# Moving two weight transfers of a kernel's opening from SyncE's queue to ScalarE's

## The chip, the cores and the metric

The kernel runs on one core of a Trainium2 chip. The metric is the device time of one execution in microseconds. Two scales appear: the timed value (343.01 us for the profiled run of the kernel before) and the span of the trace, from its first to its last instruction (341.22 us for the same run). A transfer is *issued* by the sequencer of an engine and has *landed* with the last of the sixteen semaphore updates ("marks" below) that a trace records for it; what needs its data can start then. TensorE is PE, its weight loads PEld, ScalarE ACT, VectorE DVE, SyncE SP; "SPq" and "ACTq" are the sequencers that issue transfers.

## The reference

Two independent attention blocks, A and B, side by side. Each projects 512 tokens to 32 heads of 128, attends over cached keys and values (4 key heads, 8 query heads each), and projects back. bfloat16 throughout.

```python
q = (x @ wq).reshape(B, Sq, Hq, Dh).transpose(0, 2, 1, 3)   # x: 16 x 32 x 1024, wq: 1024 x 4096
scores = einsum("bhqd,bhkd->bhqk", q, repeat(k_cache)) * Dh ** -0.5
o = einsum("bhqk,bhkd->bhqd", softmax(scores), repeat(v_cache))
out = o.transpose(0, 2, 1, 3).reshape(B, Sq, Hq * Dh) @ wo
# the outputs of A and B are concatenated
```

## The kernel before

Only the opening matters: the query projection of A's first eight heads. x has eight chunks of 128 columns; chunks 0 to 3 are loaded plainly and transposed on TensorE, chunks 4 to 7 are transposed by DMA. "Row r" below means rows r*128 to r*128+127 of wq, six heads wide (128 partitions x 768 elements, 192 KB). `NF` is 6, `HC` 4, `TT` 4, `DC` 8.

```python
def load_x(d0, t0, t1, eng=nc.sync):
    eng.dma_start(out=x_sb[:, t0:t1, d0 * P:(d0 + 2) * P],
                  in_=x_v[:, t0:t1, d0 * P:(d0 + 2) * P])

def load_w0(d0, d1, h0, h1):
    nc.sync.dma_start(out=w0[d0 // HC][:, d0 % HC:(d1 - 1) % HC + 1, h0 * DH:h1 * DH],
                      in_=wq_v[:, d0:d1, h0 * DH:h1 * DH])

load_x(0, TT // 2, TT, nc.scalar)          # x chunks 0, 1: second half of the tokens
nc.scalar.preload_act_table_set("natural_log_exp_and_others")
load_x(0, 0, TT // 2)                      # x chunks 0, 1: first half
load_w0(0, 1, 0, NF // 2)                  # first row, first half
load_w0(0, 1, NF // 2, NF)                 # first row, second half
load_w0(1, 2, 0, NF)                       # second row
load_x(2, 0, TT)                           # x chunks 2, 3
load_w0(2, 3, 0, NF)                       # third row
load_w0(3, 4, 0, NF)                       # fourth row
load_w0(0, HC, NF, REP)                    # heads 6, 7 of the first four rows
# ... the rest of the weights, x's chunks 4 to 7, keys and values, all on nc.sync
# ...
warm_up(22)
for k, ts in enumerate(((0, TT // 2), (TT // 2, TT))):
    transpose_x(0, *ts, nc.vector.tensor_copy)
    transpose_x(1, *ts, nc.scalar.copy, spare[k])
for ts in ((0, TT // 2), (TT // 2, TT)):
    first_heads(range(0, NF // 2), (0,), *ts)      # first row, first half
first_heads(range(NF // 2, NF), (0,))              # first row, second half
first_heads(range(0, NF - 2), (1,))                # second row, four heads
transpose_x(2, 0, TT, nc.vector.tensor_copy)       # x chunk 2
transpose_x(3, 0, TT, nc.scalar.copy)              # x chunk 3
first_heads(range(NF - 2, NF), (1,))               # second row, two heads
first_heads(range(NF), (2, 3))                     # third and fourth row
# ...
```

TensorE runs these in this order, so each transfer has a moment by which it must have landed.

Of the kernel before, what the change touches and what calls it, by code (L numbers as in the profile page):

```python
# [181 lines left out]
def kernel(  # L182
# [14 lines left out]
    nc = tc.nc  # L197
# [20 lines left out]
    def fast_path(ok_i):  # L218
        with ExitStack() as fctx:
# [235 lines left out]
            NF = REP - 2  # L455
# [8 lines left out]
            def load_x(d0, t0, t1, eng=nc.sync):  # L464
                eng.dma_start(
                    out=x_sb[:, t0:t1, d0 * P:(d0 + 2) * P],
                    in_=x_v[:, t0:t1, d0 * P:(d0 + 2) * P],
                )
# [4 lines left out]
                    in_=A_x.flatten_outer_dims()[:, d0 * P:(d0 + 2) * P],  # L473
                )

            def load_w0(d0, d1, h0, h1):
                nc.sync.dma_start(
                    out=w0[d0 // HC][:, d0 % HC:(d1 - 1) % HC + 1, h0 * DH:h1 * DH],
                    in_=wq_v[:, d0:d1, h0 * DH:h1 * DH],
                )  # L480

            load_x(0, TT // 2, TT, nc.scalar)
            nc.scalar.preload_act_table_set("natural_log_exp_and_others")
            load_x(0, 0, TT // 2)
            load_w0(0, 1, 0, NF // 2)
            load_w0(0, 1, NF // 2, NF)
            load_w0(1, 2, 0, NF)
            load_x(2, 0, TT)
            load_w0(2, 3, 0, NF)
            load_w0(3, 4, 0, NF)  # L490
            load_w0(0, HC, NF, REP)
            load_w0(HC, HC + 1, 0, REP)
# [182 lines left out]
    ok_i = flag.tile([1, 1], I32, name="ok_i")  # L675
    total = 2 * 2 * NG * QW
    ok = fast_path(ok_i)
    with tc.If(ok < total, preferred_fallthrough_block=True, label="general"):
        general_path(tc, problems, out_flat)
# [30 lines left out]
```

## Time and profile before

| | before |
|---|---|
| timed, median of 3 before the prediction | 343.63 us (343.56 to 343.73) |
| span of the profiled run | 341.22 us |
| TensorE busy | 335.2 us, 98% |
| first matmul of the main stream (line 301) | 18.91 us |

The lines that carry this are in the prediction below. A row of the timeline merges like instructions; its busy time hides gaps shorter than the modelled length of a matmul, so distances between starts are quoted from single records.

### The profile page before, as it was taken

How to read it: one execution, taken by the hardware profiler on the slowest of the kernel's cores; microseconds unless marked ns; L12 is line 12 of the kernel's file. 1: busy time of each engine (PE TensorE's matmuls, PEld its weight loads, DVE VectorE, ACT ScalarE, POOL GpSimd, SP SyncE). 2: the span in 40 equal slices, each digit the busy share in tenths (PEclk: the TensorE clock that was granted, in tenths of full speed). 3: DMA queues.
4: the chain of work that ended last, by engine and by line, in shares of the span. 5: the costliest groups of instructions: out<-in, count | busy, mean ns of one | idle time of the engine just before them, and what ended most of it. 6: DMA issues, size and time to landing. Idle time of an engine off the chain costs nothing.

```text
span 341.2 us, 5454 instructions
## 1 busy us (share of the span) xinstructions
PE 335.2 (98%) x2082; PEld 213.6 (63%) x2121; DVE 265.5 (78%) x336; ACT 185.9 (54%) x209; POOL 46.7 (14%) x206
## 2 busy tenths in 40 slices
PE   8999999999999999999999999999999999999996
PEld 6455666666666666666666666666666666666555
DVE  1046988888988898888888988879888888889540
ACT  3058666666667667666645545555555555555110
POOL 0001110011111111110012221222122101111100
PEclk9999999999999999999999999999999999999999
DMA  7999999999996987899999955998449997430001
GB/s 211 287 190 273 285 249 202 233 242 268 291 248 154 232 242 219 210 314 299 308 306 258 250 125 144 334 268 242 118 103 296 356 187 176 104 97 16 18 18 33
DMA packets 128094, 71.70 MB, mean 210 GB/s; under 512 B 75840, under 2 KB 127296, under 8 KB 128064
## 3 DMA queue, kind: packets, MB, share of 16 engines
q1 hardware_dynamic: 127264, 70.07, 84.1%
q0 software_dynamic: 384, 1.05, 0.9%
q8 instruction: 17, 0.28, 0.3%
q10 hardware_dynamic: 416, 0.20, 0.2%
q14 instruction: 13, 0.11, 0.1%
HBM read 50.86 MB, written 2.10 MB: 155 GB/s over the span
## 4 chain that ended last, share of the span: by engine, by line
PE 98%; issue 1%; ACT 0%; ACTq 0%
PE f_ps L320 32%; PE q_ps L301 28%; PE ob L425 17%; PE s_ps L357 16%; PE q_ps L534 4%; PE q_ps L516 1%; PE xT_ps L524 0%; ACT o_sb L329 0%; ACTq L329 0%
## 5 line engine op out<-in xcount | busy, mean ns | idle before, releaser
L365 ACT ACTIVATE p_sb<-s_ps,shift 128x1024 bf16<-128x1024 f32 x128 | 142.7, 1115 | 97.5 <-PE s_ps L357 88.1
L376 DVE TRANSPOSE_TENSOR_REDUCE parts<-p_sb 128x32 f32<-128x1024 bf16 x128 | 158.7, 1240 | 21.0 <-ACT p_sb L365 19.3
L320 PE MATMUL f_ps<-wo_sb,oT 128*128 128x512 bf16 (+1 forms) x525 | 128.2, 366 | 0.6
L301 PE MATMUL q_ps<-xT,wq_sb 128*128 128x512 bf16 x430 | 113.2, 379 | 0.5
L425 PE MATMUL ob<-p_sb,v_sb 128*128 128x256 bf16 x512 | 76.8, 273 | 0.8
L357 PE MATMUL s_ps<-qT,kT 128*128 128x256 bf16 x512 | 76.8, 273 | 0.0
L320 PEld LDWEIGHTS <-oT 128*128 128x128 bf16 x544 | 53.2, 98 | 35.3
L357 PEld LDWEIGHTS <-kT 128*128 128x128 bf16 x512 | 56.9, 113 | 28.3
L301 PEld LDWEIGHTS <-wq_sb 128*128 128x128 bf16 x448 | 43.8, 98 | 32.2
L425 PEld LDWEIGHTS <-v_sb 128*128 128x128 bf16 x512 | 50.1, 98 | 20.0
L447 DVE TENSOR_TENSOR oT<-r,ob 128x512 bf16<-128x512 f32 x64 | 43.9, 686 | 19.9 <-PE ob L425 19.4
L411 DVE STREAM_TRANSPOSE r<-rall 128x512 f32<-128x512 f32 x64 | 44.2, 691 | 1.1
L309 ACT CAST qT<-q_ps 128x512 bf16<-128x512 f32 x56 | 32.7, 583 | 16.5 <-PE q_ps L301 16.5
L394 POOL COPY half<-cs 64x32 f32<-64x32 f32 x32 | 6.5, 204 | 231.8 <-DVE cs L384 231.8
L329 ACT CAST o_sb<-f_ps 128x512 bf16<-128x512 f32 (+1 forms) x17 | 9.5, 559 | 23.6 <-PE f_ps L320 23.6
L534 PE MATMUL q_ps<-xT,w_sb 128*128 128x512 bf16 (+1 forms) x65 | 14.4, 379 | 0.1
L384 DVE TENSOR_REDUCE cs<-parts 128x32 f32<-128x128 f32 x32 | 12.1, 377 | 1.1
L406 DVE RECIPROCAL rall<-sums 128x32 f32<-128x32 f32 x32 | 10.2, 319 | 3.3 <-POOL sums L403 3.3
L534 PEld LDWEIGHTS <-w_sb 128*128 128x128 bf16 x67 | 6.8, 102 | 7.0 <-DMA w_sb<-in_A_wq_dram 0.2
L560 DVE CAST qT<-q_ps 128x512 bf16<-128x512 f32 x4 | 2.5, 684 | 10.2 <-PE q_ps L534 10.2
L331 POOL DMA_DIRECT2D out_dram<-o_sb x8 | 4.6, 574 | 29.3 <-ACT o_sb L329 29.3
L395 POOL TENSOR_TENSOR half<-half,cs 64x32 f32<-64x32 f32 x32 | 7.8, 243 | 2.6
(25 smaller groups left out, 44.7 us busy)
## 6 DMA issues: line engine op xcount, KB each, us to landing
v_sb<-in_A_v_cache_dram SPq DMA_DIRECT2D x16, 512.0 KB, 5.7
wq_sb<-in_B_wq_dram SPq DMA_DIRECT2D x8, 1024.0 KB, 5.7
wo_sb<-in_A_wo_dram SPq DMA_DIRECT2D x8, 1024.0 KB, 7.4
v_sb<-in_B_v_cache_dram SPq DMA_DIRECT2D x16, 512.0 KB, 4.7
wo_sb<-in_B_wo_dram SPq DMA_DIRECT2D x8, 1024.0 KB, 8.1
wq_sb<-in_A_wq_dram SPq DMA_DIRECT2D x5, 1024.0 KB, 5.8
wq_sb<-in_A_wq_dram SPq DMA_DIRECT2D x2, 512.0 KB, 6.7
kT<-in_A_k_cache_dram SPq DMA_TRANSPOSE x64, 4.4
```

What stands on the lines that cost most here:

```text
L301: nc.tensor.matmul(ps[:], lhsT=w[:, dc, (h % 4) * DH:(h % 4 + 1) * DH], rhs=xT[pr][:, dc, :], start=(dc == 0), stop=(dc == DC - 1),)
L309: nc.scalar.copy(out=qT[pr, g][:, :, hl, :], in_=ps[:].rearrange("p (b s) -> p b s", s=SQ),)
L320: nc.tensor.matmul(ps[:, 0:width], lhsT=oT[pr, tt][:, h, :], rhs=wo_tiles[pr, nh, h // REP][:, h % REP, off:off + width], start=(h == 0), ...
L357: nc.tensor.matmul(s_ps[:, c, :], lhsT=kT[:, i % GRP, c, :], rhs=qT[pr, g][:, b, :, :].rearrange("p h s -> p (h s)"), start=True, stop=True,)
L365: nc.scalar.activation(out=p_sb[:], in_=s_ps[:], func=ACTF.Exp, bias=shift[:], scale=SCALE)
L376: nc.vector.tensor_reduce(out=parts[k][:, q, :, :].rearrange("p c h -> p (c h)"), in_=st[i]["p"][:].rearrange("p c (h s) -> p (c h) s", s=SQ),
L384: nc.vector.tensor_reduce(out=cs[:], in_=parts.pop(k)[:].rearrange("p q c h -> p q h c"), axis=AX.X, op=ALU.add,)
L406: nc.vector.reciprocal(out=rall[:, k, :], in_=quad.pop(k)[:])
L411: nc.vector.transpose(out=r[:].rearrange("p n s -> p (n s)"), in_=rall[:, k, o * 2 * REP:(o + 1) * 2 * REP] .unsqueeze(2).to_broadcast([P, ...
L425: nc.tensor.matmul(ob[j][:, q, :], lhsT=v_sb[:, i % GRP, c, :], rhs=st[i]["p"][:, c, :], start=(c == 0), stop=(c == KC - 1),)
L447: nc.vector.tensor_tensor(out=out, in0=rcp.pop(j)[:].rearrange("p (q h) s -> p q h s", h=REP), in1=ob.pop(j)[:].rearrange("p q (h s) -> p ...
L534: nc.tensor.matmul(first_q[h][:, ts], lhsT=w0[dc // HC][:, dc % HC, h * DH:(h + 1) * DH], rhs=xT[0][:, dc, ts], start=(dc == 0 and t0 == 0 ...
```

## The change

The intent: SyncE issues one transfer each 0.47 us or so, and the opening's transfers stand in its queue. ScalarE has only its part of x and a table load to do at first. Giving it the second and third rows should bring these sooner, and let SyncE get on about a microsecond earlier.

```diff
-            def load_w0(d0, d1, h0, h1):
-                nc.sync.dma_start(
+            def load_w0(d0, d1, h0, h1, eng=nc.sync):
+                eng.dma_start(
...
             load_w0(0, 1, NF // 2, NF)
-            load_w0(1, 2, 0, NF)
+            load_w0(1, 2, 0, NF, nc.scalar)
             load_x(2, 0, TT)
-            load_w0(2, 3, 0, NF)
+            load_w0(2, 3, 0, NF, nc.scalar)
             load_w0(3, 4, 0, NF)
```

## The prediction

> **What bounds the kernel now.** I read the head of the page first, then the chain of waits, then only the first ten microseconds, since every moved transfer belongs to the opening.
>
> From the page of the kernel before:
>
> ```profile
> span 341.2 us, 5454 instructions
> PE 335.2 (98%) x2082; PEld 213.6 (63%) x2121; DVE 265.5 (78%) x336; ACT 185.9 (54%) x209; POOL 46.7 (14%) x206
> ...
> PE 98%; issue 1%; ACT 0%; ACTq 0%
> ```
>
> The second line gives each engine's busy time, the third the chain of work that ended last. TensorE is busy 335.2 of 341.2 us and is 98% of that chain; no transfer appears in it. A transfer that lands earlier can pay only where TensorE waits for it. So I listed all waits of TensorE's weight loads over the whole span:
>
> ```profile
> PEld L516 <- issue: 0.9, 1, 0.9
> PEld L534 <- DMA w_sb<-in_A_wq_dram: 0.2, 1, 0.2
> ```
>
> Columns: who waited, for what, total us, times, longest. One weight load in the whole program waits for a weight transfer, 0.2 us. That is a row the change moves, so the hope behind the change has a target. The timeline shows whether those 0.2 us reach the matmuls (start, length, engine, line, out<-in, count, idle time before it):
>
> ```profile
> 0.93 2.52 PE L516 MATMUL q_ps<-const-bfloat16-1.0 128*128 128x128 bf16 x22 [0.93 <-PEq L694]
> ...
> 3.28 1.09 PE L524 MATMUL xT_ps<-ident,x_sb 128*128 128x128 bf16 x8
> ...
> 4.17 2.79 PE L534 MATMUL q_ps<-xT,w_sb 128*128 128x256 bf16 x13
> ...
> 5.79 0.67 PEld L534 LDWEIGHTS <-w_sb 128*128 128x128 bf16 x4 [0.20 <-DMA w_sb<-in_A_wq_dram]
> ...
> 6.79 0.61 PE L524 MATMUL xT_ps<-ident,x_sb 128*128 128x128 bf16 x8
> ...
> 7.45 11.62 PE L534 MATMUL q_ps<-xT,w_sb 128*128 128x512 bf16 x52
> ```
>
> None of these matmul rows has an idle time but the first. In the single records the distances between matmul starts tell more than the busy rows. Around the waiting load, matmuls start at 5.710, 5.925, 6.141, 6.357 us: each 0.215 us after the last, the undisturbed distance of a 512-column matmul in this trace. The load ran beside the previous matmul, so its 0.2 us cost nothing. Real losses before 8 us are three:
>
> - the first transpose of x at 3.276 instead of 3.241 (0.035 us; SyncE's half of x landed at 3.23),
> - the fifth at 3.763 instead of 3.678 (0.085 us; ScalarE's half landed at 3.72),
> - 0.024 us at 7.690, where the matmul waits for VectorE's copy of the third x chunk.
>
> The other gaps near 0.22 us later on are each one missing matmul record. So TensorE is paced by its own instructions from 4.165 us to the end.
>
> **How tight each row is.** From issue, landing and first weight load (single records and issues of the trace):
>
> - first row, first half (96 KB): issued 1.26, landed 3.92, loaded at 4.06: 0.14 us to spare
> - first row, second half (96 KB): 1.75, 5.03, 5.17: 0.14
> - second row (192 KB): 2.22, 5.75, 5.79: none for the load, which still kept pace
> - x chunks 2 and 3 (256 KB): 2.69, 6.55, 6.59: almost none
> - third row (192 KB): 3.17, 7.06, 7.45: 0.4
> - fourth row (192 KB): 3.71, 7.77, 8.77: 1.0
> - everything behind: 0.9 us or more (the next block landed 9.13, its matmuls start near 10.05).
>
> The order was already tuned to arrive just in time. The change touches the tight ones.
>
> **What the Trainium skill says.** "DMA: Bandwidth & Descriptors", section "Issuing engines are not separate DMA queues", says that DMAs started from several engines run on the same 16 engines and interleave, and that this saves only issue time. The trace agrees: the two x halves are issued side by side (0.74 and 0.82 us, 0.45 and 0.46 us long), but SyncE's packets start at 1.83 and ScalarE's only at 2.51 us, when SyncE's are nearly done. "Perfetto Trace Analysis", section "Sequencer Loop", says engine instructions are pushed into a queue while the sequencer goes on reading. The trace agrees for short waits: at 338.24 us ScalarE's sequencer finishes a semaphore wait inside its cast of 338.22 to 338.59. No record shows a DMA issued during a table load. "ScalarE: Activation LUTs", section "What ACT_TABLE_LOAD costs", gives about 1283 ns for the load, and this trace has 1.28 us, from 1.31 to 2.60; the drain that it adds is not visible here, since ScalarE's next instruction waits for TensorE. "TensorE: Matmul & The Clock Gate", Part 1, says matmuls run at half clock until about 4 us of activity; here 256-column starts lie 0.213 us apart until 5.02 us, and 512-column ones 0.215 us apart from about 5.3 us, so the full rate comes about 4.1 us after the first warm-up matmul at 0.93.
>
> **The change part by part.** TensorE, VectorE and GpSimd keep the same instructions in the same order. SyncE loses two issues; ScalarE gains two, behind its x half and the table load. In the listing of the changed program the transfers keep their places in the ring of eight completion semaphores, so the waits are the old ones.
>
> 1. SyncE saves 0.476 us before x chunks 2 and 3 (2.690 less 2.215) and 0.547 us more before the fourth row (the spacing 3.166 to 3.713): 1.02 us for all behind. All these were hidden: gain on the path 0.
>
> 2. The second and third rows' issue on ScalarE. If the sequencer passes the table load, they go at about 1.31 and 1.78 us instead of 2.22 and 3.17. Landings come 0.5 to 1 us sooner, and the 0.2 us wait of the load may vanish: gain 0, since the matmuls kept pace.
>
> 3. Contention for the first row. Its second half (issued 1.75) would now have the second row's 192 KB beside or ahead of it. DMA was not full there: 117 and 163 GB/s in 3.5 to 4.5 us, where 348 GB/s is reached in 5.0 to 5.5. Estimate from these: 96 + 96 + 192 KB from its first packet at 2.89 us at some 300 GB/s take 1.3 us, so all three end near 4.2; landings trail most of the packets by 0.6 to 0.8 us, giving 4.8 to 5.0. Serial handling as between the two x halves could add 0.65 us (192 KB at 300 GB/s) to the 5.03: at worst 5.6 against a need of 5.17. I take 5.2 to 5.4 as likely, a stall of 0 to 0.25 us. The first half, if pushed back 0.1 us, has 0.14 to spare.
>
> 4. x's own halves are issued before everything moved, so the two losses of 0.035 and 0.085 us remain. At most 0.024 us can come back at 7.690, and that needs an earlier copy, while its transposes keep their place: 0.
>
> Sum: 0 gained, about 0.1 us lost in the mean: 343.63 + 0.1 = 343.73, rounded up slightly for the second rival.
>
> **The rivals.**
>
> *A small gain.* The labelled 0.2 us wait could be taken at face value: 343.4. For it: it is the only transfer wait of TensorE's weight loads. Against it: the even 0.215 us distances across it, and the start still hangs on x.
>
> *ScalarE's sequencer waits out the table load.* Then the rows go at about 2.60 and 3.07 us. The second row is issued 0.38 us later than before and behind x chunks 2 and 3, now issued at 2.22. It would land 0.4 to 0.8 us later than 5.75, or 0.4 to 0.8 us of stall with nothing else to absorb it: 344.0 to 344.4. Separate queues would soften this. The copies of xT on ScalarE, first due at 3.92, would still be free of it: two issues of about 0.47 us end near 3.55. I give this 30%, because the trace has no DMA beside a table load.
>
> *Contention as in part 3 at its worst.* 0.45 us on the first row's second half: 344.1. For it: the serial packets of the two x halves. Against it: the DMA engines' share was only 0.53 at 3.5 to 4.0 us.
>
> *A reordering far downstream.* Buffers and waits are unchanged, TensorE never waits for data later, so no cost beyond the opening has anything to hang on.
>
> **Range and chances.** The three runs before differ by 0.17 us. All mechanisms lie between -0.15 us (all three start-up losses gone) and +0.8 us; 2% is 6.9 us, over eight times the largest of them. I predict 343.8 us, 343.3 to 344.4, and leave 1% for each side of the 2% band.
>
> **What would show each step.** Issue times of the second and third rows on ScalarE: near 1.3 and 1.8 us (part 2) or near 2.6 and 3.1 (rival). The first row's second half landing before 5.17 us means no stall; later shows part 3. A gap over 0.215 us between matmul starts from 5.1 to 6.6 us is the whole change in time. SyncE's fourth-row issue should come at about 2.69. The start of the first 512-column q_ps matmul of the main stream (18.9 us) should move by the same amount as the span. What would make me wrong: a change of span without such a gap in the opening, an earlier landing of x itself, or a full clock that comes at another time because the opening's waits shifted.

## The result, and the profile after

| | before, same rounds | after |
|---|---|---|
| timed, median | 343.60 us (343.02 to 343.73) | 344.02 us (343.52 to 345.30) |
| ratio of the means | | 1.0018, 95% interval 1.0000 to 1.0036 |
| span of the profiled run | 341.22 us | 341.74 us |
| first matmul of the main stream | 18.91 us | 19.44 us |

A ratio here is one of means of runs of the same rounds, so not quite the ratio of the medians. (The ratios for the experiments below come out if the first run of each kernel in the set is left out; where means are compared in words, all runs are in.) By the 2% rule the two are the same, and the interval begins at 1.0000: the loss is at the edge of what these runs can tell. Five of the six runs after are at 343.5 to 344.0 us, one is at 345.3.

The head of the page and the chain of waits of the changed kernel:

```profile
span 341.7 us, 5493 instructions
...
PE 97%; DMA 1%; SPq 0%; ACT 0%; issue 0%; ACTq 0%
PE f_ps L320 32%; PE q_ps L301 28%; PE ob L425 16%; PE s_ps L357 16%; PE q_ps L534 3%; DMA x_sb<-in_A_x_dram 1%; SPq L477 0%; PE xT_ps L524 0%; SPq L465 0%; ACT o_sb L329 0%; ACTq L329 0%
```

A transfer is now on the chain that sets the end, and it is none of the two that were moved: it is x. (The higher instruction count comes from matmul records missing in the first trace, not from more work: the weight loads are 2121 in both.) All waits of the weight loads, over the whole span:

```profile
PEld L516 <- issue: 0.9, 1, 0.9
PEld L524 <- DMA x_sb<-in_A_x_dram: 0.9, 1, 0.9
PEld L534 <- DMA w_sb<-in_A_wq_dram: 0.7, 2, 0.4
```

And the timeline (start, length, engine, line, out<-in, count, idle before):

```profile
1.31 1.28 ACT L483 ACT_TABLE_LOAD   x1 [1.31 <-PEq L694]
1.34 0.93 ACTq L477 DMA_DIRECT2D w_sb<-in_A_wq_dram  x2
2.22 0.43 SPq L465 DMA_DIRECT2D x_sb<-in_A_x_dram  x1
...
4.25 0.55 PEld L534 LDWEIGHTS <-w_sb 128*128 128x128 bf16 x6 [0.27 <-DMA w_sb<-in_A_wq_dram]
...
5.23 1.19 PEld L534 LDWEIGHTS <-w_sb 128*128 128x128 bf16 x7 [0.43 <-DMA w_sb<-in_A_wq_dram]
...
7.30 0.62 PE L524 MATMUL xT_ps<-ident,x_sb 128*128 128x128 bf16 x8 [0.38 <-DMA x_sb<-in_A_x_dram]
```

The first two rows show ScalarE issuing both rows inside its table load, at 1.34 and 1.83 us. The third shows x chunks 2 and 3 issued at 2.22, where the kernel before had 2.69. The last shows their transposes at 7.30 us instead of 6.79, after a wait for exactly this transfer. It was issued 0.47 us earlier and landed 0.71 us later: 7.26 us instead of 6.55. The span is longer by the same 0.52 us as the transposes are later. The chain in order of time says it in one line (start, length, what):

```profile
2.22 5.04 DMA x_sb<-in_A_x_dram
7.26 0.05 issue
7.30 0.62 PE xT_ps L524 x8
```

Landings (single records), with the moment each is needed in the kernel before:

| transfer | needed | before: issued, landed | after: issued, landed |
|---|---|---|---|
| first row, first half | 4.06 | 1.26, 3.92 | 1.25, 4.20 |
| first row, second half | 5.17 | 1.75, 5.03 | 1.75, 5.19 |
| second row | 5.79 | 2.22, 5.75 | 1.34 (ScalarE), 4.99 |
| x chunks 2 and 3 | 6.59 | 2.69, 6.55 | 2.22, 7.26 |
| third row | 7.45 | 3.17, 7.06 | 1.83 (ScalarE), 6.55 |
| fourth row | 8.77 | 3.71, 7.77 | 2.69, 7.81 |

What was not yet needed came sooner (third row), what was needed next came later (x). The clock is not the reason in this run: it was full from 3.80 us, and from 5.09 in the kernel before. Behind the fourth row, SyncE's sequencer now has a wait that the kernel before does not have (waits of SyncE in the first 12 us):

```profile
SPq L477 <- DMA x_sb<-in_A_x_dram: 0.5, 1, 0.5
```

Its next issue is at 3.67 us, 0.02 us after ScalarE's half of x landed, instead of 4.19: what stands behind the fourth row is issued 0.52 us earlier. How full the DMA engines were, in the same stretches, before and then after (stretch, length, busy time of PE, PEld, DVE, ACT, POOL, clock, DMA share, GB/s):

```profile
1.80:3.30 1.50, 1.50 (x17) 1.41 (x15) 0.00 (x0) 0.80 (x1) 0.00 (x0) 1.00 0.80 243
3.30:4.60 1.30, 1.30 (x13) 1.02 (x12) 0.58 (x2) 0.57 (x2) 0.00 (x0) 1.00 0.70 147
4.60:6.40 1.80, 1.80 (x11) 1.05 (x10) 0.00 (x0) 0.18 (x1) 0.00 (x0) 1.00 1.03 339
1.80:6.40 4.60, 4.60 (x36) 3.48 (x34) 0.58 (x2) 1.54 (x3) 0.00 (x0) 1.00 0.86 253
```

```profile
1.80:3.30 1.50, 1.50 (x16) 1.38 (x13) 0.00 (x0) 0.80 (x1) 0.00 (x0) 1.00 0.74 218
3.30:4.60 1.30, 1.21 (x14) 0.94 (x13) 0.58 (x2) 0.63 (x2) 0.00 (x0) 1.00 1.02 324
4.60:6.40 1.80, 1.64 (x11) 0.76 (x9) 0.00 (x0) 0.01 (x1) 0.00 (x0) 1.00 0.93 282
1.80:6.40 4.60, 4.35 (x36) 3.08 (x34) 0.58 (x2) 1.44 (x3) 0.00 (x0) 1.00 0.89 273
```

The second queue did fill a hole: 324 GB/s instead of 147 in 3.3 to 4.6 us. But after that the engines were full in the kernel before (share 1.03) and nearly so in the changed one (0.93), and over 1.8 to 6.4 us the gain is 20 GB/s, 92 kB in 4.6 us. The third row is 197 kB, and it is now ahead of x. An estimate from these: the missing 105 kB at 340 GB/s are 0.3 us of the 0.71 us by which x is later. The sixteen marks of this transfer fit that: the middle one (mean of the eighth and the ninth) moved by 0.2 us, from 6.13 to 6.35, the last by 0.71. The rest is that the last marks trail further behind in this run, and why is not told by the trace.

### The profile page after: what moved, and what is told of

The parts are those of the page before. It is cut to its first block, busy times and chain, and to the rows that moved or that the text cites. A ratio compares the mean times of both kernels' runs of the same rounds, so it can differ in the third digit from the quotient of the medians.

```text
span 341.7 us, 5493 instructions
## 1 busy us (share of the span) xinstructions
PE 337.1 (99%) x2121; PEld 212.9 (62%) x2121; DVE 265.6 (78%) x336; ACT 185.7 (54%) x209; POOL 46.6 (14%) x206
## 4 chain that ended last, share of the span: by engine, by line
PE 97%; DMA 1%; SPq 0%; ACT 0%; issue 0%; ACTq 0%
PE f_ps L320 32%; PE q_ps L301 28%; PE ob L425 16%; PE s_ps L357 16%; PE q_ps L534 3%; DMA x_sb<-in_A_x_dram 1%; SPq L477 0%; PE xT_ps L524 0%; SPq L465 0%; ACT o_sb L329 0%; ACTq L329 0%
## 5 line engine op out<-in xcount | busy, mean ns | idle before, releaser
L320 PE MATMUL f_ps<-wo_sb,oT 128*128 128x512 bf16 (+1 forms) x544 | 132.3, 367 | 0.0
L301 PE MATMUL q_ps<-xT,wq_sb 128*128 128x512 bf16 x448 | 117.0, 379 | 0.0
```

Source lines behind the costliest of these rows:

```text
L301: nc.tensor.matmul(ps[:], lhsT=w[:, dc, (h % 4) * DH:(h % 4 + 1) * DH], rhs=xT[pr][:, dc, :], start=(dc == 0), stop=(dc == DC - 1),)
L320: nc.tensor.matmul(ps[:, 0:width], lhsT=oT[pr, tt][:, h, :], rhs=wo_tiles[pr, nh, h // REP][:, h % REP, off:off + width], start=(h == 0), ...
```

## The experiments

Twelve experiments ran (some of them a kernel once more), in three sets of four on one chip each, every one timed in five rounds against the kernel before. Theory A: the third row's bytes get ahead of x chunks 2 and 3, whose landing sets the end. Rivals: the first row suffers beside the second queue (rival 1, later theory B: by rare slow landings); the full clock of TensorE comes at another time (rival 2); two issuing engines cost by themselves. Edits are shown against the changed kernel unless said otherwise.

**1. Only the second row on ScalarE (twice).**

```diff
-            load_w0(2, 3, 0, NF, nc.scalar)
+            load_w0(2, 3, 0, NF)
```

> Only the second row stays on ScalarE; the third row is issued by SyncE behind x chunks 2 and 3 again. Theory (the loss is the third row's 192 KB getting ahead of x chunks 2 and 3): these chunks land near 6.4 us, 6.6 at most, instead of 7.26; the transposes at 6.6 to 6.85; time within 0.2 us of the kernel before (343.4 to 343.8). Rival 1 (the first row delayed by the second row beside it is the loss): the first row still lands at 4.2 and 5.2 us as in the changed kernel, and the time stays 0.3 to 0.5 us above before. Rival 2 (the full clock comes at another time): the time follows the clock, whatever x does.

Measured: median 343.20 us (342.96 to 343.99), ratio 0.9998 (0.9985 to 1.0011). x chunks 2 and 3 landed at 6.22 us, their transposes started at 6.74. The whole list of what TensorE's weight loads waited for in this run has one line left, and the transposes carry no wait:

```profile
6.74 0.61 PE L524 MATMUL xT_ps<-ident,x_sb 128*128 128x128 bf16 x8
```

As theory A has it, the third row behind x gives the time back (the median even lies under the 343.4 to 343.8 expected). This is the cleanest of the comparisons: x is issued at 2.22 us as in the changed kernel, and only the third row's place differs. Rival 1 predicted a loss that is not there; the first row landed at 3.88 and 5.12 us here, so the second row beside it did no harm in this run. The repetition:

> Only the second row on ScalarE, once more, for a firmer size. Theory A: x chunks 2 and 3 land at 6.2 to 6.6 us, the mean is 0.1 to 0.3 us under the kernel before (it was 0.14 under). If the first time was luck, it is equal to before within 0.1 us, with the landing near 7.1.

Measured: five runs at 343.42 to 343.54 and one at 345.12; ratio 1.0008 (0.9991 to 1.0025). x landed early again (6.13 us), but now the third row landed at 8.05 us and its matmuls waited:

```profile
8.09 0.82 PE L534 MATMUL q_ps<-xT,w_sb 128*128 128x512 bf16 x3 [0.27 <-DMA w_sb<-in_A_wq_dram]
```

So the early landing of x came again, and the small lead over the kernel before did not. No gain shows in these two sets; in this trace the lateness moved to the next transfer.

**2. Only the third row on ScalarE.**

```diff
-            load_w0(1, 2, 0, NF, nc.scalar)
+            load_w0(1, 2, 0, NF)
```

> Only the third row on ScalarE, issued near 1.35 us; the second row by SyncE behind the first. Theory: the third row still gets ahead, now of the second row as well: x chunks 2 and 3 land at 7.0 to 7.4 us, the transposes start there, time 0.3 to 0.6 us above before. Rival 1: the first row has as many bytes beside it as in the changed kernel, so the same loss as there by another way; the theory is told from it by where matmuls stand idle longest: at the transposes of x chunks 2 and 3 (theory) or only at the first row (rival).

Measured: median 343.58 us, ratio 1.0005 (0.9992 to 1.0019): the means differ by 0.17 us, less than the 0.3 expected and not clear of noise. x chunks 2 and 3 landed at 7.30, the transposes started at 7.35, span 341.79: where theory A puts them, and x is issued at 2.69 us as in the kernel before. The sign that was to tell rival 1 apart, the place of the longest idle time, does not decide: by the distances of matmul starts, 0.19 us are lost at the first row's second half and 0.19 us at the transposes.

**3. One queue, one swap.** The kernel before with nothing on ScalarE but its part of x, and the third row ahead of x on SyncE. This takes away the second queue; x, however, is also issued one place later, at 3.16 us instead of 2.69.

```diff
 # against the kernel before
-            load_x(2, 0, TT)
             load_w0(2, 3, 0, NF)
+            load_x(2, 0, TT)
```

> The kernel before with one swap on SyncE: the third row ahead of x chunks 2 and 3, nothing on ScalarE but its part of x. Theory A: x chunks 2 and 3 land 0.5 to 0.7 us later than in the kernel before, with a gap there; time up by 0.3 to 0.6 us, as in the changed kernel. Theory B: only one queue, so no sharing with the first row; time as before within 0.2 us, and no run at 345 us or more.

Measured: median 343.94 us (343.77 to 344.33), ratio 1.0014 (1.0000 to 1.0028), means 0.43 us apart. x landed at 7.61 us, 1.06 and 0.50 us later than in the two traces of the kernel before (0.5 to 0.7 expected):

```profile
7.65 0.62 PE L524 MATMUL xT_ps<-ident,x_sb 128*128 128x128 bf16 x8 [0.31 <-DMA x_sb<-in_A_x_dram]
```

This costs what the change costs, without a second queue. How much of it is the order of the bytes and how much the later issue, this run does not tell; in experiments 1 and 2 the issue time of x is that of the kernel compared with. No run reached 345 us.

**4. The cost doubled.** The fourth row, too, ahead of x.

```diff
+            load_w0(3, 4, 0, NF)
             load_x(2, 0, TT)
             load_w0(2, 3, 0, NF, nc.scalar)
-            load_w0(3, 4, 0, NF)
```

> The changed kernel with the suspected cost doubled: the fourth row's 192 KB, too, ahead of x chunks 2 and 3, on SyncE. Theory A: x chunks 2 and 3 land 0.5 to 0.7 us later than in the changed kernel (7.8 to 8.0), the time is 0.8 to 1.2 us above before. Theory B: sharing of the first row with the other queue is the same, so the median stays where the changed kernel has it, with the same single slow runs.

Measured: median 344.37 us (344.09 to 344.86), ratio 1.0029 (1.0014 to 1.0044), means 0.93 us apart. x landed at 8.13 us (7.8 to 8.0 expected), 0.42 to 0.87 us later than in the two traces of the changed kernel; it was also issued 0.47 us later:

```profile
PE xT_ps L524 <- DMA x_sb<-in_A_x_dram: 1.1, 1, 1.1
```

TensorE stood idle 1.1 us for it. Every run lies above the median of the changed kernel. This is as theory A has it, in place and nearly in size.

**5. Both kernels once more, for the noise.**

> The kernel before against itself, for the noise and a second look at its opening. Ratio 1.000 within 0.002. If landings are steady, the opening repeats the first trace (transposes of x chunks 2 and 3 at 6.8 us, no gap over 0.1 us). If the landing times of the opening's transfers vary from run to run, as the spread of 342.7 to 343.9 hints, x chunks 2 and 3 or the first row land at another time by several tenths, and the span moves with them.

Measured: the kernel before against itself 1.0007 (0.9991 to 1.0024). Its second trace is not the first: x chunks 2 and 3 landed at 7.11 us, and the transposes started at 7.26, with a span of 341.70 us. The first profile of before, 343.01 us, lay under all six timed runs of its kernel (343.02 to 343.73).

```profile
7.26 0.61 PE L524 MATMUL xT_ps<-ident,x_sb 128*128 128x128 bf16 x8
```

This row has no wait: TensorE was late before it. Its clock came to full speed at 5.63 us in this run and at 5.09 in the first (clock records of the traces), and landings were later by 0.2 to 0.6 us; the first transposes started 0.20 us later, behind x's first half, and the second row's landing at 6.34 held up a matmul by 0.12.

> The changed kernel again. Theory A (x chunks 2 and 3 behind the third row): these land at 7.1 to 7.4 us as before, median 0.3 to 0.6 us above the kernel before. Theory B (the first row's second half shares each DMA engine with two rows of the other queue, and a slow read there holds it up, rarely but for long): the median is nearly that of before and the mean is raised by single runs of 345 us and more, as in 1 of 6 and 2 of 6 runs so far.

Measured: median 343.90 us (343.46 to 344.20), ratio 1.0009 (0.9994 to 1.0023). x landed at 7.71 us and the transposes waited until 7.75; span 342.19. No run at 345 us. The loss of the change is thus 0.3 us in this set (means) and 0.6 in the first, of which 0.2 are the single run at 345.3; neither is clear of noise by its interval.

**6. The wait for x taken away (wrong result), in both kernels.** The transposes of chunks 2 and 3 read chunks 0 and 1; the transfer of 2 and 3 still runs. (The record marks these runs as correct all the same, so its check did not see the edit.)

```diff
-                        ps[:, tt * P:(tt + 1) * P], x_sb[:, tt, d * P:(d + 1) * P], ident[:]
+                        ps[:, tt * P:(tt + 1) * P], x_sb[:, tt, (d % 2) * P:(d % 2 + 1) * P], ident[:]
```

In the changed kernel:

> Wrong result on purpose: the changed kernel, but the transposes of x chunks 2 and 3 read chunks 0 and 1, so that nothing waits for the transfer of chunks 2 and 3, which still runs. Theory: the gap of 0.55 us at the transposes goes, and the time comes back by 0.4 to 0.5 us, to that of before or up to 0.2 us under it, limited by the first row (5.2 us) and the third (6.55). Rival 1: the first row's delay stays and so does the time, 0.3 to 0.5 us above before.

Measured: 343.07, 343.27, 343.55, 344.15, 346.12 and 346.76 us; ratio 1.0018 (0.9992 to 1.0044). Not what theory A expected. The profiled run was the one at 346.76:

```profile
4.27 0.83 PE L534 MATMUL q_ps<-xT,w_sb 128*128 128x256 bf16 x6
7.25 3.10 PE L534 MATMUL q_ps<-xT,w_sb 128*128 128x512 bf16 x7 [2.15 <-DMA w_sb<-in_A_wq_dram]
```

The first row's second half landed at 7.20 us instead of 5.19, and TensorE stood idle over 2 us. What that does to its clock shows in the stretches of this run (clock is the third column from the right):

```profile
4.00:5.00 1.00, 0.96 (x10) 0.56 (x7) 0.36 (x2) 0.64 (x2) 0.00 (x0) 1.00 0.76 223
...
7.50:10.50 3.00, 3.00 (x11) 1.26 (x10) 0.00 (x0) 0.00 (x0) 0.00 (x0) 0.50 1.22 202
11.00:12.00 1.00, 0.95 (x7) 0.42 (x5) 0.24 (x1) 0.59 (x1) 0.00 (x0) 1.00 1.07 364
```

Half clock from 7.35 to 10.77 us: the gap cost over 2 us, and the slow clock after it half of 3.41 us more. Once more, with the control on the kernel before:

> Wrong result on purpose: the changed kernel without the wait for x chunks 2 and 3, once more, with other timings. Theory A: without single slow runs the times lie at 343.0 to 343.5, under the changed kernel's 343.9 to 344.0. Theory B: one to three of the six runs lie at 345 us or more again.

Measured: 343.17, 343.50, 344.06, 344.59, 344.63 and 346.69 us; ratio 1.0032 (1.0006 to 1.0059). The profile fell on the run at 343.50. There the transposes started at 7.17 us, 0.30 us before x landed (7.47), and the span was 341.60: in this trace the time did come back.

> Wrong result on purpose, and the control of the earlier run without this wait: the kernel before, with the transposes of x chunks 2 and 3 reading chunks 0 and 1. Theory A: in those runs of the kernel before where chunks 2 and 3 land late they set the end, so the mean falls by 0.1 to 0.4 us and no run lies more than 0.1 us above the median of before. Theory B (sharing of the first row with the other queue makes the runs of 345 us and more): none here, since there is one queue.

Measured: 343.01 to 343.96 us, ratio 0.9990 (0.9977 to 1.0003). In the kernel before, taking the wait away costs nothing and may gain 0.2 us. In the changed kernel it does not bring the mean back: something else is late in a part of the runs, and three of twelve lie above 346 us. One of these three is seen to be the first row's second half; the other two have no trace, and their mean granted clock is 1.000 (0.995 in the first), so no loss of clock as in the first is visible in them. The runs at 344.1 to 344.6 have no trace either.

**7. A version in the order of need (twice).** Only the first row's second half on ScalarE; everything behind it in its old order, one issue earlier.

```diff
-            load_w0(0, 1, NF // 2, NF)
-            load_w0(1, 2, 0, NF, nc.scalar)
+            load_w0(0, 1, NF // 2, NF, nc.scalar)
+            load_w0(1, 2, 0, NF)
             load_x(2, 0, TT)
-            load_w0(2, 3, 0, NF, nc.scalar)
+            load_w0(2, 3, 0, NF)
```

> A version built from the theory: ScalarE issues only the first row's second half behind its part of x; second row, x chunks 2 and 3, third row stay in the order of need on SyncE, each one issue (about 0.47 us) earlier. Theory: x chunks 2 and 3 land near 6.2 to 6.5 us, the first row's second half no later than 5.1; no stall over 0.1 us; time equal to before or up to 0.3 us under it (343.2 to 343.7). Rival (two issuing engines cost by themselves, by interleaving): x chunks 2 and 3 land past 6.8 us and the time is 0.2 us or more above before.

Measured: median 343.48 us, ratio 1.0004 (0.9991 to 1.0017). The time was within what was expected, the landing was not: x came at 7.26 us, with the same bytes ahead of it as in experiment 1. Fifteen of its sixteen marks had come by 6.37 us; the last was 0.89 us behind them.

> Only the first row's second half on ScalarE, once more, since x chunks 2 and 3 landed at 7.26 us there against the 6.2 to 6.5 expected. If that landing was chance, they land under 6.8 us now and the mean falls 0.1 us or more under before; if it belongs to this order, they land at 7.1 to 7.4 again and the time stays at that of before.

Measured: median 343.46 us, ratio 1.0002 (0.9988 to 1.0015). x landed at 6.67 us this time, so 7.26 does not belong to the order. Yet the transposes started at 7.53, without a wait: the clock was full only at 6.68 us. This version is no faster than the kernel before, and of the twelve runs none is by more than its interval.

### What the traces say together

"Clock full from" is the first clock record of a trace. Before it, matmuls of 256 columns start 0.213 us apart, after it 0.109.

| kernel | clock full from | x chunks 2, 3 landed | their transposes start | span | span less start |
|---|---|---|---|---|---|
| before | 5.09 | 6.55 | 6.79 | 341.22 | 334.43 |
| before, again | 5.63 | 7.11 | 7.26 | 341.70 | 334.44 |
| second row on ScalarE | 5.07 | 6.22 | 6.74 | 341.18 | 334.44 |
| second row on ScalarE, again | 4.96 | 6.13 | 6.79 | 341.64 | 334.85 |
| order of need | 5.33 | 7.26 | 7.31 | 341.75 | 334.44 |
| order of need, again | 6.68 | 6.67 | 7.53 | 341.96 | 334.43 |
| third row on ScalarE | 5.14 | 7.30 | 7.35 | 341.79 | 334.44 |
| after | 3.80 | 7.26 | 7.30 | 341.74 | 334.43 |
| after, again | 6.19 | 7.71 | 7.75 | 342.19 | 334.44 |
| swap on one queue | 3.67 | 7.61 | 7.65 | 342.09 | 334.44 |
| fourth row ahead, too | 5.17 | 8.13 | 8.18 | 342.61 | 334.43 |

Eleven traces, and in ten the span is 334.43 to 334.44 us after the first transpose of x chunks 2 and 3; the one exception is the run where the third row's landing waited behind it. So the start of these transposes is the end of the opening, and two things set it: the landing of x (starts 0.04 to 0.05 us after a landing) or TensorE's own work, which is later when the full clock or the earlier landings come later. With the third row behind x, x landed at 6.13 to 7.26 us in six traces (mean 6.66); with it ahead, at 7.26 to 7.71 in four (mean 7.47); with two rows ahead, at 8.13. The three traces of experiment 6, left out of the table, fit: 7.19 behind, 7.47 and 8.08 ahead.

The last mark scatters, the middle one less, and it parts the two orders at the same issue time. Issued at 2.22 us, x has its middle mark at 5.45 to 6.19 us in the four traces with the third row behind it, and at 6.35 to 6.82 in the four with the third row ahead; issued at 2.69, at 6.13 to 6.42 in three traces behind, and at 6.78 in experiment 2. In the changed kernel the third row's own middle mark is at 5.36 us, before x's 6.35; in experiment 1 it is at 6.02, after x's 5.45. So the third row did overtake x, and x is later where it does.

## Why the prediction was right, and where it was not

The time was right: 343.8 predicted, 343.3 to 344.4 as the range, 344.02 and later 343.90 measured, and the same within 2%. The cause was named only half, and that the number came so near is in part luck: 343.8 was 343.63 plus 0.1 us for the first row, rounded up, and the loss came from a term taken as 0.

- **No gain, since the one labelled wait cost nothing.** Right. The second row landed 0.76 us sooner and the third 0.51, within the "0.5 to 1 us sooner", and no run gained from it. The rival that took 0.2 us at face value is not borne out.
- **ScalarE's sequencer passes the table load.** Right: the issues are at 1.34 and 1.83 us, "about 1.31 and 1.78" predicted. The rival in which it waits out the table load falls.
- **SyncE saves 0.476 us before x chunks 2 and 3; "gain on the path 0".** The issue moved as predicted, 2.69 to 2.22 us, and so did the fourth row's (2.69); those behind it came 0.52 us earlier, not the 1.02 summed, since a wait that was said to be the old one now held them. But this step took an earlier issue for no harm. It is the step that failed: the moved third row got ahead of x in the DMA engines, and x landed 0.71 us later in the first pair of traces. The prediction listed x as having "almost none" to spare and then sought the contention only at the first row. Experiment 1 shows the order of the bytes as the cause: with x issued at the same 2.22 us and the third row behind it, x landed at 6.22 and 6.13 us instead of 7.26 and 7.71. Experiments 3 and 4 bear it out in time, with x issued 0.47 us later as well: a swap on one queue costs 0.43 us, a second row ahead 0.93.
- **Contention at the first row, "a stall of 0 to 0.25 us".** The second half landed at 5.19 and 5.52 us, just outside the 5.2 to 5.4 called likely on either side, the first half at 4.20 against 4.06 needed, which had been called safe. (The worst case, 5.03 plus 0.65, is 5.68, not 5.6.) TensorE's weight loads idled 0.27 and 0.43 us for the two. These stalls are real but stand ahead of the later wait for x and are covered by it: the span follows x. The prediction's worst case took the two halves of x, which were served nearly one after the other, as a pattern; in the changed kernel packets of both queues run side by side from 3.3 to 5 us.
- **"A gap over 0.215 us between matmul starts from 5.1 to 6.6 us is the whole change in time."** The sign was sought too early: the gap that sets the span is that before the transposes, from 6.76 us, where they would have followed, to 7.30. That the first matmul of the main stream moves with the span was right (0.53 and 0.52 us).
- **The size.** About 0.1 us of loss was summed; measured 0.6 us (first set) and 0.3 (second). The term that was mis-sized is the delay of x, taken as 0: in the first pair of traces x landed 0.71 us later and its transposes started 0.52 us later.
- **"TensorE is paced by its own instructions from 4.165 us to the end."** True of that trace, not of the kernel. The start of the full clock between 3.67 and 6.97 us over all traces, and landings that vary by half a microsecond, move the opening of the kernel before by nearly as much as the change does (0.47 us between its two traces). This blurs the loss: in the trace whose clock came at 6.68 us, the transposes started at 7.53 with x landed at 6.67.

What stays open. Single runs over 345 us came in 5 of the 57 runs of kernels with at least one weight row on ScalarE and in none of the 56 with all of them on SyncE. One such run was traced, with the first row's second half 2 us late; fifteen of its sixteen marks were there by 5.98 us, the last came at 7.20. That would fit a share of the DMA engines with the other queue's rows, but no experiment isolated it. Why taking away the wait for x did not bring the changed kernel's time back in its middle runs is not settled either; so "x sets the end" is shown for the two traced runs of the changed kernel, and for the changed kernel it is not the only thing that can.

## What to carry to other kernels

An issue saved on one queue is not a transfer saved: where the DMA engines are full, moving a transfer to an idle queue moves it ahead of something, so list what it will overtake and how much that has to spare. A wait label on a weight load is no loss if the matmul starts keep their distance. And where an opening is tuned to arrive just in time, one profile is one draw: take a second profile of the kernel before, against which to hold the one after.

## What the Trainium skill lacked or had wrong

- "DMA: Bandwidth & Descriptors", section "Issuing engines are not separate DMA queues", says that a second issuing engine saves only sequencer time. The section lacks the other side: the order of service changes. (The page tells elsewhere how an engine shares itself between queues, but not this consequence and no number for it.) x chunks 2 and 3, issued 0.47 us earlier, landed 0.71 us later in the first pair of traces, as the third row overtook them.
- "ScalarE: Activation LUTs", section "What ACT_TABLE_LOAD costs", does not say whether ScalarE can issue transfers meanwhile; only the general rule that the prediction cites covers it. It can: two issues at 1.34 and 1.83 us inside a table load of 1.31 to 2.60. The load's 1.28 us agree with the page; the drain that it adds shows in no trace here.
- "TensorE: Matmul & The Clock Gate", Part 1, gives about 4 us of activity with 0.5 us of scatter until the full clock. With the first matmul at 0.93 us in every trace, it came at 3.67 to 6.97 us, so 2.7 to 6.0 us after it. That section's free-running window of 3.4 us fits this spread better than its 0.5 us. Its table gives half clock after at least one idle window of about 3.4 us. Here a gap in the matmuls of some 2.2 us (start distance 2.42 us, one run) was followed by half clock for 3.41 us, so a gap shorter than that window can be enough.
- No page has this, and it is a point of the profile's views, not of the chip: the clock column of a stretch shows 1.00 before the trace's first clock record, though the matmuls run at half speed: before 5.02 us 256-column matmuls start 0.213 us apart under a column of 1.00.
